# Tuned linear attention and a feed-forward layer on one core: a third group of the first product goes to seven quarter products, two of its sums share one pair of PSUM banks, q is loaded in longer runs, and the order of the work is a written list

## The chip, the core and the metric

The kernel runs on one core of a Trainium2 chip. Times are device microseconds (us) of that core, from one launch to its end; the figure that counts is the median of several runs. A profiled execution gives, beside its own time, a trace: the span from its first to its last instruction, with every instruction of the engines in it. The engines are PE (matrix products; PEld is its weight load), DVE (vector), ACT (scalar), POOL and SP. POOL and SP mostly issue DMAs here. Each engine works through its instructions in order, and a wait at one instruction holds up all behind it on that engine.

## What is computed

Eight batches with eight heads of 576 tokens and 64 channels go through attention without a softmax, then a normalization, then two matrix products with a leaky step between them. Cut to what matters:

```python
kv  = einsum('bhsd,bhse->bhde', k, v)            # q, k, v: (8, 8, 576, 64)
o   = einsum('bhsd,bhde->bhse', q, kv)
x   = (o / sqrt(mean(o*o, -1) + 1e-6) * g_norm)  # heads side by side: (4608, 512)
h   = x @ w_in                                   # the first product, 512 -> 2048
g   = maximum(h, 0) + alpha * minimum(h, 0)      # the gate
out = g @ w_out                                  # the second product, 2048 -> 512
```

## The kernel before

The 4608 tokens are cut into nine blocks of 512, w = 0 to 8. Blocks 0 and 1 are written out as straight code. From block 2 on every piece of work is a step: `put_m1`, `put_attention`, `put_m2`, `put_moves` and `put_rest` (L1450 to L1760) list them with what they need, and `in_order` (L1875) emits them. Before the change it takes, of the steps that are ready, the one with the lowest due time in the table `AT` (L1774). The order in which steps are emitted is the order of the instructions on every engine, since the pools are under a manual schedule.

The first product has 16 output tiles of 128 features in a block, in four groups s = 0 to 3. A plain tile (`put_tile`, steps M, r, s) is four matmuls of 512 columns into one PSUM bank (L641), then ACT writes relu(-h) to `m_sb` (L650), then DVE forms the gated result `gt` (L656). A fast group (`put_fast`, from block 3 on for s = 2 and 3) makes the four tiles of a group with seven products of quarters instead of eight (steps f.w.s.n): each is four matmuls of 256 columns (L1247). Products 1, 6, 7 and 4 are summed in a bank Y, 2 in a bank X, 5 and 3 in a bank V. Between them ACT copies the state of Y: `seed` (into X, before 6 changes Y), `u2` (after 6) and `u3` (after 7). DVE forms the other two quarters as `c22` = V + u3 after product 5, and `c12` = V + u2 after product 3 (L1269), both into tiles `mh` in SBUF. All four quarters are then gated 256 columns at a time: ACT copy (L1307), two DVE steps (L1314). The sums of quarters of x and w_in that the products need are the steps t and a.

Four banks serve the first product: h1 and h2 of one pool, m0 and m1 of another, each m bank a tile of its own. They go round: a fast group takes Y, V and X from the list `hs`, which is then turned over, so that the next group gets other banks.

The second product (steps p, L895) uses seven quarter products over sums of `gt` (steps S); a step p is four matmuls of 256 columns. Steps y read its banks, steps st store the result.

For attention, POOL issues the loads of k, v and q (steps ld). Each load is preceded by a one-element copy on POOL, a gate (L1402), that waits for a recent `gt`, so that loads don't start too early. q comes in four loads of 128 tokens (`load_q`, L209), each in runs of 64 channels; SP turns each by a DMA transpose (steps q, L400) into `qt_sb`. Steps kv and kvc make the per-head matrix; steps R (L519) make the rows of o, q2 and q3 their squares on ACT, rs the root, n the scaling on DVE, x the transpose by SP into `xt` for the next block. SP also issues some stores of results.

The last block ends with the second product's last quarter and its stores.

Of the kernel before, what the change touches and what calls it, by code (L numbers as in the profile page):

```python
# [17 lines left out]
def kernel(  # L18
# [11 lines left out]
    nc = tc.nc  # L30
# [178 lines left out]
    def load_q(b, t):  # L209
        if (b, "q") not in stages:  # L210
            stages[b, "q"] = stage_for(b, "q", [P, TPP, H, D])
        nc.gpsimd.dma_start(  # L212
            out=stages[b, "q"][:, t, :, :],
            in_=srcs["q"][b, :, t * P : (t + 1) * P, :].rearrange("h p d -> p h d"),
        )
# [176 lines left out]
    def dma_t(b, ts=tuple(range(NT))):  # L392
        qt = qt_sb[b % 2][:, :, PAD : PAD + S]
        for t in ts:
            c0, c1 = t * P, min((t + 1) * P, S)
            if t == TPP:
                src = rem_of(b, "q")[0:REM]
            else:
                src = buf_of(b, "q")[:, t] if b < B_NAT else stages[b, "q"][:, t]
            nc.sync.dma_start_transpose(  # L400
                out=qt[:, :, c0:c1], in_=src.rearrange("p h d -> p (h d)"),
            )
        for j in range(NPAIR):
            qts[b, j] = qt_sb[b % 2][:, j, PAD : PAD + S]

# [99 lines left out]

    def rows_mm(w, tiles):
        o_ps = row_tile([2, 2, NPAIR, D], "or_ps")
        for x, i in enumerate(tiles):
            b, r = divmod(w * W + i * P, S)
            for j in range(NPAIR):  # L510
                if r + P <= S:
                    steps = ((b, PAD + r),)
                else:
                    assert r + PAD == S
                    steps = ((b, S), (b + 1, 0))
                for n, (bb, c) in enumerate(steps):
                    for h in range(2):
                        part = slice(h * D, (h + 1) * D)
                        nc.tensor.matmul(  # L519
                            out=o_ps[:, h, x, j, :],  # L520
                            lhsT=qt_sb[bb % 2][part, j, c : c + P],
                            rhs=kvs[bb, j][part, part],
                            start=(n == 0), stop=(n == len(steps) - 1), skip_group_check=True,
                        )
            ots[w, "r", i] = o_ps[:, :, x]
# [100 lines left out]
    gt_last = []  # L626
    h_turn = [0]
# [72 lines left out]
    def row_pieces(n0):  # L700
        i = 0
        while i < P:
            b, r = divmod(n0 + i, S)
            np_, nt = (P0, T0) if b == 0 else (P, TPP)
            if b < B_NAT and r < np_ * nt:
                t, p = divmod(r, np_)
                cnt = min(P - i, np_ - p)
                yield i, cnt, b, t, p
            else:
                cnt = P - i if b >= B_NAT else min(P - i, S - r)  # L710
                yield i, cnt, None, n0 + i, 0
            i += cnt
# [186 lines left out]
    def quad_out(w, r, h, src, subs=(0, 1)):  # L899
        n0 = w * W + r * HW  # L900
        if n0 >= B_NAT * S and len(subs) == 2:
            put(
                out[n0 : n0 + HW, h * HC : (h + 1) * HC].rearrange("(a p) m -> p a m", p=P),
                src[:],
            )
            return
# [286 lines left out]
    M1_FROM = {2: 3, 3: 3}  # L1193
    HD = NC // 2
    spare, xsums, m1s = {}, {}, {}
    SPARE = {1: "q", 2: "k", 3: "v"}
    hs = ["h2", "h1", "m0", "m1"]
# [10 lines left out]
    def a_sum(s, n, pool=0):  # L1208
        if s not in spare:
            spare[s] = stage_tile(SPARE[s], [P, 4, HD, 2 * P])  # L1210
# [48 lines left out]
    def m1_step(w, s, what, tags):  # L1259
# [7 lines left out]
        elif what in ("c22", "c12"):  # L1267
            src, u = (t["V"], t["u3"]) if what == "c22" else (t["V"], t["u2"])
            nc.vector.tensor_add(out=h_tile(t, what)[:, :, HW:W], in0=src[:], in1=u[:])  # L1269
        elif what in ("a11", "a21"):  # L1270
            src = t["X"] if what == "a11" else t["Y"]
            nc.scalar.copy(out=h_tile(t, what)[:, :, 0:HW], in_=src[:])
        elif what[1] in "AB":
            i = s + (what[1] == "B") * KQ
            r = int(what[2])
            h = t["h" + what[1]]
            if what[0] == "r":
                t["m" + what[1:]] = m_new(h[:, r, :])
                return
            m1_out(w, i, r, slice(0, W), t["m" + what[1:]][:], h[:, r, :])  # L1280
            gt_add(w, i, 2)
        else:
            f_half, t_half = int(what[1]) - 1, int(what[2]) - 1
            cols = slice(t_half * HW, (t_half + 1) * HW)
            if t_half == 0:
                h = t["X" if f_half == 0 else "Y"][:]
            else:
                h = t["hB" if f_half else "hA"][:, :, HW:W]
# [3 lines left out]
            i = s + f_half * KQ  # L1292
# [4 lines left out]

    def h_tile(t, what):
        nm = "hA" if what in ("c12", "a11") else "hB"
        if nm not in t:  # L1300
            t[nm] = u_p.tile([P, 2, W], FP32, name="mh", bufs=2)
        return t[nm]
# [7 lines left out]
    def m1_out(w, i, r, cols, m, h):  # L1310
        if (w, i) not in gts:
            gts[w, i] = gt_tile(w, i)
        g = 2 * i + r
        nc.vector.scalar_tensor_tensor(  # L1314
            out=gts[w, i][:, r, cols], in0=m, scalar=beta_sb[:, g : g + 1], in1=h,
            op0=ALU.mult, op1=ALU.add,
        )
        gt_last[:] = [gts[w, i][0:1, r, cols.start : cols.start + 1]]
# [26 lines left out]
    def kv_copy(b):  # L1345
        for i in range(2):
            part = slice(i * D, (i + 1) * D)
            nc.scalar.copy(out=kv_masked[part, b % 4, :, part], in_=kv_tiles[b][part])
# [77 lines left out]
    def load(nm, b):  # L1426
        if nm == "q":
            for t in range(TPP):
                load_q(b, t)
# [7 lines left out]
    planned.append(1)  # L1437

# [21 lines left out]
    def put_fast(w, s):  # L1460
        tags = dict(Y=hs[0], V=hs[1], X=hs[2])
        hs[:] = [hs[3], hs[2], hs[1], hs[0]]
# [18 lines left out]
        do("c22", "tt", key("u3"), key(5), take=("h", w, s, "B"))  # L1481
        mm(3, key("c22"), ("a", s, 4))
        do("c12", "tt", key(3), key("u2"), take=("h", w, s, "A"))
        done = {}
        for half, p1, p2, n in (("A", "11", "12", 2), ("B", "21", "22", 4)):
            old_gt = ("gt", w - 2, s + KQ * (half == "B"))
            if whole(w, s, half):
                do("a" + p1, "copy", key(n), key("c" + p2))
                for r in range(2):
                    m = ("m", w, s, half, r)  # L1490
                    do(f"r{half}{r}", "relus", key("c" + p2), key("a" + p1), take=m)
                    do(f"s{half}{r}", "stt", key(f"r{half}{r}"), old_gt,
                       free=(m, ("h", w, s, half)) if r else (m,))
                done[half] = key(f"s{half}0"), key(f"s{half}1")
                done[p1] = key("a" + p1)
            else:
                for x, p in enumerate((p1, p2)):
                    m = ("m", w, s, p)
                    do("r" + p, "relus" if x else "relu", key("c" + p2) if x else key(n), take=m)
                    do("s" + p, "stt2", key("r" + p), old_gt, free=(m, ("h", w, s, half)) if x else (m,))  # L1500
                done[half] = key("s" + p1), key("s" + p2)
                done[p1] = key("s" + p1)
        bank_free[tags["Y"]] = done["21"], key(4)
        bank_free[tags["V"]] = (key("c12"),)
        bank_free[tags["X"]] = (done["11"],)
# [31 lines left out]
    def put_m2(w):  # L1537
# [17 lines left out]

        full = lambda f, k: f(k) + f(k + 1) if pairs else f(k)
        for k in range(0, 4, 2 if pairs else 1):
            if w > 1:
                sums(3, k, *full(lo, k), *used(7, k))
            sums(1, k, *full(lo, k), *full(hi, k), *used(5, k))  # L1560
            sums(2, k, at(1, k), *used(6, k))
# [105 lines left out]
    def put_rows(w, tiles, free, used):  # L1667
        needs = []
        for i in tiles:
            b, r = divmod(w * W + i * P, S)  # L1670
            needs += [("q", b, t) for t in range(r // P, min((r + P - 1) // P, TPP) + 1)]
            needs.append(("kvc", b))
            if r + P > S:
                needs += [("q", b + 1, 0), ("kvc", b + 1)]
# [16 lines left out]
    def put_moves(w):  # L1691
        b = w + 1
        for t in range(NT if b < B else 0):
            step(("q", b, t), "turn", lambda t=t: dma_t(b, (t,)),
                 (("ld", "q", b, t), *(("R", b - 1, i) for i in (1, 3))))
# [5 lines left out]
    def turned(what, w, i):  # L1701
        if what == "x":
            return xts[w][0:1, 0, i * P : i * P + 1]
        return qt_sb[w % 2][0:1, 0, PAD + i * P : PAD + i * P + 1]
# [7 lines left out]
    def put_load(nm, b):  # L1712
        needs = (("kv", b - 1),) if nm != "q" else ()
        for t in range(NT) if nm == "q" else (TPP, 0):
# [12 lines left out]
            own = (("q", b - 2 if t == TPP else b - 1, t),) if nm == "q" else ()  # L1727
            step(("ld", nm, b, t), "part" if t == TPP else "loadq" if nm == "q" else "load", fn, needs + own + after)

    def put_rest():  # L1730
# [12 lines left out]
        for w in range(min(M1_FROM.values()), NW):  # L1743
            for n in range(1, 5):
# [3 lines left out]
                     (*x_all(w), *((("t", w, n // 2),) if n in (2, 4) else ()), *used))  # L1748

    LATE_KV = 4  # L1750

    def whole(w, s, half):
        return False
# [23 lines left out]
    LOOP = 27.0  # L1777
    AT = {
# [160 lines left out]
```

## Time and profile before

| | us |
|---|---|
| median of the runs | 272.12 |
| the runs | 271.74, 274.9, 272.12 |
| the profiled execution's own time | 270.98 |
| its span | 269.2 |
| PE busy | 261.9 |
| DVE busy | 228.1 |
| ACT busy | 191.8 |
| POOL busy | 94.9 |

The 1.8 us between own time and span lie before the first and after the last instruction. A busy time counts the union of an engine's instructions. [...] In a timeline row stand the start, the length, engine and line, the tile written and the tiles read, and the number of equal instructions in the row; in brackets the idle time before it and what ended that.

### The profile page before, as it was taken

How to read it: one execution, taken by the hardware profiler on the slowest of the kernel's cores; microseconds unless marked ns; L12 is line 12 of the kernel's file. 1: busy time of each engine (PE TensorE's matmuls, PEld its weight loads, DVE VectorE, ACT ScalarE, POOL GpSimd, SP SyncE). 2: the span in 40 equal slices, each digit the busy share in tenths (PEclk: the TensorE clock that was granted, in tenths of full speed). 3: DMA queues.
4: the chain of work that ended last, by engine and by line, in shares of the span. 5: the costliest groups of instructions: out<-in, count | busy, mean ns of one | idle time of the engine just before them, and what ended most of it. 6: DMA issues, size and time to landing. Idle time of an engine off the chain costs nothing.

```text
span 269.2 us, 6788 instructions
## 1 busy us (share of the span) xinstructions
PE 261.9 (97%) x2477; PEld 182.8 (68%) x2477; DVE 228.1 (85%) x437; ACT 191.8 (71%) x684; POOL 94.9 (35%) x166
## 2 busy tenths in 40 slices
PE   6999999999999999999999999999999999999994
PEld 2554454456556757885788678867885788678883
DVE  6559966899977888999889988998899989978962
ACT  2567637787579779879977997799779983757400
POOL 8853652513530326874346521804040003002100
PEclk9999999999999999999999999999999999999999
DMA  7999999995999899999999993999464013100413
GB/s 189 201 199 206 195 198 189 183 195 92 195 128 169 75 131 126 129 161 197 189 163 156 138 153 66 110 191 129 107 138 99 19 24 119 39 2 11 145 41 118
DMA packets 90821, 35.76 MB, mean 133 GB/s; under 512 B 62996, under 2 KB 88612, under 8 KB 90788
## 3 DMA queue, kind: packets, MB, share of 16 engines
q0 software_dynamic: 57104, 23.68, 68.5%
q1 hardware_dynamic: 32708, 10.63, 24.0%
q10 hardware_dynamic: 976, 1.02, 1.2%
q8 instruction: 19, 0.31, 0.5%
q14 instruction: 14, 0.11, 0.2%
HBM read 36.71 MB, written 9.44 MB: 171 GB/s over the span
## 4 chain that ended last, share of the span: by engine, by line
PE 85%; DMA 8%; ACT 2%; issue 2%; DVE 1%; SPq 1%; POOL 0%; POOLq 0%
PE h_ps L641 23%; PE yY L895 14%; PE yX L895 9%; PE yZ L895 8%; PE mY L1247 8%; PE y L686 5%; PE mV L1247 4%; DMA qt_sb<-qst 3%; PE h_ps L674 2%; DMA vst<-in_v_dram 2%; PE mX L1247 2%; PE or_ps L519 1%; DMA y_sb<-in_g_norm_dram 1%; DMA qst<-in_q_dram 1%; PE kv_ps L1337 1%
## 5 line engine op out<-in xcount | busy, mean ns | idle before, releaser
L641 PE MATMUL h_ps<-xt,w_in_sb 128*128 128x512 f16 x348 | 83.0, 379 | 0.1
L656 DVE SCALAR_TENSOR_TENSOR gt<-m_sb,beta_sb,h_ps 128x512 f16<-128x512 f32 x96 | 67.1, 741 | 4.6 <-ACT m_sb L650 3.6
L650 ACT ACTIVATE m_sb<-h_ps 128x512 f32<-128x512 f32 x96 | 55.0, 604 | 14.3 <-PE h_ps L641 11.9
L641 PEld LDWEIGHTS <-w_in_sb 128*128 128x128 f16 x348 | 33.1, 98 | 32.3 <-issue 0.3
L895 PEld LDWEIGHTS <-s 128*128 128x128 f16 x496 | 48.0, 98 | 8.4 <-DVE s L813 0.2
L895 PEld LDWEIGHTS <-gt 128*128 128x128 f16 x384 | 37.4, 98 | 8.6
L582 ACT ACTIVATE sq_sb<-or_ps 128x64 f16<-128x64 f32 x192 | 39.7, 286 | 2.2 <-PE or_ps L519 2.2
L582 ACT ACTIVATION_READ_ACCUMULATOR sq_sb<-or_ps 128x1 f32 x192 | 39.4, 273 | 0.0
L1402 POOL COPY gate_sb<-gt 1x1 f16<-1x1 f16 x39 | 10.5, 269 | 76.9 <-DVE gt L656 54.7
L895 PE MATMUL yX<-w_out_sb,gt 128*128 128x256 f16 x256 | 35.2, 273 | 0.0
L895 PE MATMUL yY<-wsum,s 128*128 128x256 f16 x256 | 32.9, 273 | 0.0
L698 POOL DMA_DIRECT2D out_dram<-y_sb x24 | 15.2, 639 | 45.8 <-ACT y_sb L957 42.8
L608 DVE TENSOR_TENSOR x_rows<-or_ps,rstd_r 128x512 f16<-128x512 f32 x27 | 17.4, 685 | 9.0 <-ACT rstd_r L592 8.8
L1314 DVE SCALAR_TENSOR_TENSOR gt<-m_sb,beta_sb,mh 128x256 f16<-128x256 f32 x48 | 20.5, 477 | 0.2 <-ACT m_sb L1307 0.2
L1307 ACT ACTIVATE m_sb<-mh 128x512 f32<-128x512 f32 x24 | 15.1, 629 | 6.3 <-DVE mh L1269 6.3
L1266 ACT COPY mu<-mY 128x512 f32<-128x512 f32 x24 | 14.1, 588 | 6.5 <-PE mY L1247 6.5
L1269 DVE TENSOR_TENSOR mh<-mV,mu 128x512 f32<-128x512 f32 x24 | 16.4, 685 | 2.5 <-ACT mu L1266 2.4
L212 POOL DMA_DIRECT2D qst<-in_q_dram x20 | 17.8, 891 | 2.2 <-issue 2.0
L686 PE MATMUL y<-w_out_sb,gt 128*128 128x512 f16 x64 | 16.3, 380 | 0.0
L895 PE MATMUL yZ<-wsum,s 128*128 128x256 f16 x120 | 16.2, 273 | 0.0
L895 PE MATMUL yY<-wsum,gt 128*128 128x256 f16 x128 | 15.5, 273 | 0.0
L1247 PEld LDWEIGHTS <-w_in_sb 128*128 128x128 f16 x144 | 14.1, 98 | 1.6
(150 smaller groups left out, 425.0 us busy)
## 6 DMA issues: line engine op xcount, KB each, us to landing
kst<-in_k_dram POOLq DMA_DIRECT2D x7, 512.0 KB, 7.7
vst<-in_v_dram POOLq DMA_DIRECT2D x6, 512.0 KB, 6.5
out_dram<-y_sb POOLq DMA_DIRECT2D x11, 256.0 KB, 3.2
qst<-in_q_dram POOLq DMA_DIRECT2D x20, 128.0 KB, 4.5
w_out_sb<-in_moe_w_out_dram POOLq DMA_DIRECT2D x8, 256.0 KB, 12.1
out_dram<-y_more POOLq DMA_DIRECT2D x5, 256.0 KB, 4.2
w_in_sb<-in_moe_w_in_dram POOLq DMA_DIRECT2D x2, 512.0 KB, 10.4
qst<-in_q_dram POOLq DMA_DIRECT2D x2, 512.0 KB, 10.7
```

The costliest lines, as they stand in the source:

```text
L212: nc.gpsimd.dma_start(out=stages[b, "q"][:, t, :, :], in_=srcs["q"][b, :, t * P : (t + 1) * P, :].rearrange("h p d -> p h d"),)
L582: nc.scalar.activation(out=sq[:, half, j], in_=o_ps[:, half, j], func=AF.Square, accum_out=ssq[:, half, j : j + 1],)
L608: nc.vector.tensor_tensor(out=xr[:].rearrange("p j h d -> p h j d"), in0=o_ps, in1=rstd[:].unsqueeze(3).to_broadcast([P, 2, NPAIR, D]), op ...
L641: nc.tensor.matmul(out=h_ps[:], lhsT=w_in_blk(c, g), rhs=xts[w][:, c, :], start=(c == 0), stop=(c == NC - 1),)
L650: nc.scalar.activation(out=neg[w, g][:], in_=h_ps[:], func=AF.Relu, scale=-1.0)
L656: nc.vector.scalar_tensor_tensor(out=gts[w, i][:, r, :], in0=neg.pop((w, g))[:], scalar=beta_sb[:, g : g + 1], in1=h_ps[:], op0=ALU.mult, ...
L686: nc.tensor.matmul(out=y[:], lhsT=gt_cols(w, g, a * P, (a + 1) * P), rhs=w_out_blk(g), start=(n == 1), stop=(n == NF),)
L698: engs[store_turn[0] % len(engs)].dma_start(out=dst, in_=src)
L895: nc.tensor.matmul(out=bank, lhsT=lhs, rhs=rhs, start=fresh, stop=(c == NK - 1), skip_group_check=True,)
L1247: nc.tensor.matmul(out=t[bank][:, r, :], lhsT=lhs[:, c, r * P : (r + 1) * P], rhs=rhs[:, c, :], start=(fresh and c == r == 0), stop=(c == ...
L1269: nc.vector.tensor_add(out=h_tile(t, what)[:, :, HW:W], in0=src[:], in1=u[:])
L1314: nc.vector.scalar_tensor_tensor(out=gts[w, i][:, r, cols], in0=m, scalar=beta_sb[:, g : g + 1], in1=h, op0=ALU.mult, op1=ALU.add,)
```

## The change

1. `M1_FROM = {1: 4, 2: 3, 3: 3}`: group 1 is made by seven products too, in blocks 4 to 8. Five times 16 matmuls of 512 columns give way to 28 of 256, with the copies and sums of a fast group. The sums of w_in for it get a tile of their own.
2. The banks m0 and m1 become the two halves of one tile, allocated once: `m_pair`, 128 x 2 x 512. In every fast group X is m0 and V is m1; Y takes h2 and h1 in turn. Plain tiles on m0 or m1 write halves of the same tile.
3. `c12` is written back into the V half in PSUM. X and V side by side then hold both quarters of a result tile, and one ACT copy and one DVE step of 512 columns, which reach into both banks (steps rA0, sA0, rA1, sA1), gate it. `c22`, 21 and 22 are as before, with a smaller `mh`.
4. q of batches 3 to 7 is loaded in two loads of four heads, in the layout of k and v (each partition holds four tokens that follow each other, 512 bytes in a run after the cast). A transpose takes two heads with all their tokens, so the rows of one tile need all four transposes. A second copy of the per-head matrix with the halves swapped is made by `kvc` (three ACT copies instead of two). Rows where two batches meet are made in parts of 64. Outputs are stored by the new token order, in more and smaller pieces.
5. A written list `ORDER` of all steps takes the place of due times and planner. A load in it carries its gate (`@name`), or none (`@!`).

```diff
-    def load_q(b, t):
-        ...
-            out=stages[b, "q"][:, t, :, :],
-            in_=srcs["q"][b, :, t * P : (t + 1) * P, :].rearrange("h p d -> p h d"),
+    QL = 2
+    def load_q(b, i):
+        load_main(b, "q", i * H // QL, (i + 1) * H // QL)
...
     def m1_bank(tag, shape, name):
-        pool = ps_h if tag[0] == "h" else m_pool[0]
-        return pool.tile(shape, FP32, name=name, tag=tag)
+        if tag[0] == "h":
+            return ps_h.tile(shape, FP32, name=name, tag=tag)
+        bank = m_pair[:, int(tag[1])]
+        return bank if len(shape) == 2 else bank.rearrange("p (r n) -> p r n", r=shape[1])
...
-    M1_FROM = {2: 3, 3: 3}
+    M1_FROM = {1: 4, 2: 3, 3: 3}
-    hs = ["h2", "h1", "m0", "m1"]
+    hs = ["h2", "m0", "m1", "h1"]
...
-        elif what in ("c22", "c12"):
-            src, u = (t["V"], t["u3"]) if what == "c22" else (t["V"], t["u2"])
-            nc.vector.tensor_add(out=h_tile(t, what)[:, :, HW:W], in0=src[:], in1=u[:])
+        elif what == "c22":
+            t["h"] = u_p.tile([P, 2, HW], FP32, name="mh", bufs=2)
+            nc.vector.tensor_add(out=t["h"][:], in0=t["V"][:], in1=t["u3"][:])
+        elif what == "c12":
+            nc.vector.tensor_add(out=t["V"][:], in0=t["V"][:], in1=t["u2"][:])
+        elif what[1] == "A":
             r = int(what[2])
+            h = m_pair[:, :, r * HW : (r + 1) * HW]
             if what[0] == "r":
                 t["m" + what[1:]] = m_new(h)
                 return
+            m1_out(w, s, r, slice(0, W), t["m" + what[1:]][:], h)
...
+    m_pair = m_pool[0].tile([P, 2, W], FP32, name="m_pair")
...
     def put_fast(w, s):
-        tags = dict(Y=hs[0], V=hs[1], X=hs[2])
-        hs[:] = [hs[3], hs[2], hs[1], hs[0]]
+        tags = dict(Y=hs[0], X="m0", V="m1")
+        hs[:] = hs[::-1]
...
+        for r in range(2):
+            m = ("m", w, s, "A", r)
+            do(f"rA{r}", "relu", key("c12"), key(2), take=m)
+            do(f"sA{r}", "stt", key(f"rA{r}"), old_gt, free=(m,))
...
+        bank_free[tags["V"]] = bank_free[tags["X"]] = done["A"]
...
             def fn(t=t, after=after):
-                gate(gt_last[0])
+                for src in load_gate:
+                    gate(src)
```

A stretch of the list, in block 7, where the pair of banks goes from group 2 to group 3:

```python
f.7.2.3 f.7.2.r21 f.7.2.2 f.7.2.c12 x.8.2 f.7.2.r22 p.6.5.0 n.8.3 p.6.5.1 f.7.2.rA1 p.6.2.3
f.7.2.rA0 f.7.2.sA1 x.8.3 p.6.5.2 f.7.3.1 f.7.2.sA0 p.6.5.3 f.7.2.s22 f.7.3.seed f.7.3.5
y.6.c11 f.7.3.6
```

Steps f with a number, p, M, R and kv are PE's; seed, u, r and most y are ACT's; c, s, t, S and n are DVE's; x and q are SP's, ld POOL's.

More of the change, by code (lines that the diff above doesn't have):

```diff
@@ L402, in dma_t, with qt_flat, place_of @@
             )
-        for j in range(NPAIR):
+        for j in range(NPAIR if b < B_NAT else 0):
             qts[b, j] = qt_sb[b % 2][:, j, PAD : PAD + S]
+    def qt_flat(b):
+        return qt_sb[b % 2][:].rearrange("p j n -> p (j n)")
+    def place_of(b, r):
+        if b >= B_NAT and b % 2:
+            r = r - REM if r >= REM else r + MAIN
+        return divmod(r, P) if r < MAIN else (TPP, r - MAIN)
     def unit0(i):
@@ L506, in rows_mm @@
     def rows_mm(w, tiles):
         o_ps = row_tile([2, 2, NPAIR, D], "or_ps")
+        ops = [row_ops(w, i) for i in tiles]
+        apart = all(len({y[0] for y in x}) == 1 for x in ops)
+        left = []
         for x, i in enumerate(tiles):
[L509 to L524, printed above, removed]
@@ L525, in rows_mm @@
-            ots[w, "r", i] = o_ps[:, :, x]
+            half = ops[x][0][0]
+            ots[w, "r", i] = o_ps[:, half] if apart else o_ps[:, :, x]
+            left += [(x, *op) for op in ops[x]]
+        if not apart:
+            left.sort(key=lambda y: y[3].stop - y[3].start)
+        was = None
+        while left:
+            n = next((n for n, y in enumerate(left) if was and y[1] != was[1]), 0)
+            x, half, h, rows, j, lhs, rhs = was = left.pop(n)
+            nc.tensor.matmul(
+                out=ots[w, "r", tiles[x]][rows, h, j, :], lhsT=lhs, rhs=rhs, start=True,
+                stop=True, skip_group_check=True,
+            )
@@ L1427, in load @@
         if nm == "q":
[L1428 to L1429 removed]
+            for i in range(QL):
+                load_q(b, i)
             load_rem(b, "q")
@@ new lines @@
+    """.split()
+    def in_order():
+        todo = {".".join(map(str, s[0])): s for s in steps if s[1]}
+        names, done, gates = {s[0] for s in steps if s[1]}, set(), {"-": gt_last[0]}
+        for x in ORDER:
+            name, _, at = x.partition("@")
+            s = todo.pop(name)
+            assert all(n in done or n not in names for n in s[3]), name
+            if at:
+                load_gate[:] = [gates[at]] if at != "!" else []
+            yield s[2]
+            done.add(s[0])
+            gates[name] = gt_last[0]
+        assert not todo
```

347 lines of the change are left out of this document (203 added, 144 removed), and 66 rows, old and new, of the table AT.

## The prediction

> **What bounds the kernel now.** I read the busy times, then the chain, then busy times by block, then single rows.
>
> ```profile
> PE 261.9 (97%) x2477; PEld 182.8 (68%) x2477; DVE 228.1 (85%) x437; ACT 191.8 (71%) x684; POOL 94.9 (35%) x166
> PEclk9999999999999999999999999999999999999999
> PE 85%; DMA 8%; ACT 2%; issue 2%; DVE 1%; SPq 1%; POOL 0%; POOLq 0%
> ```
>
> PE fills the span, and the chain that ended last runs on it for 85%, at full clock throughout. What PE saves is saved, and what PE waits is lost. Next the blocks 3 to 7 (PE, PEld, DVE, ACT, POOL in each stretch):
>
> ```profile
> 117.50:144.80 27.30, 26.75 (x272) 20.65 (x268) 24.07 (x46) 23.01 (x99) 14.05 (x27) 1.00 1.28 163
> 144.80:171.80 27.00, 27.00 (x278) 20.81 (x276) 24.88 (x47) 23.02 (x99) 11.52 (x23) 1.00 0.95 116
> 171.80:199.00 27.20, 27.20 (x286) 20.95 (x284) 24.92 (x47) 23.12 (x99) 7.99 (x14) 1.00 0.92 131
> 199.00:226.40 27.40, 27.40 (x248) 21.26 (x247) 26.01 (x49) 23.17 (x98) 2.65 (x4) 1.00 0.32 84
> ```
>
> A block takes about 27 us and PE has no gap, but DVE idles only 1.4 to 3.2 us and ACT about 4 us in each. This order works because every wait is covered exactly. How exactly, one place shows:
>
> ```profile
> 106.89 0.60 PE L1247 MATMUL mY<-t,kst 128*128 128x256 f16 x4
> 107.33 1.04 PE L895 MATMUL yY<-wsum,s 128*128 128x256 f16 x8
> 107.53 0.59 ACT L1266 COPY mu<-mY 128x512 f32<-128x512 f32 x1
> 108.20 0.60 PE L1247 MATMUL mY<-t,kst 128*128 128x256 f16 x4
> 116.28 0.68 DVE L1269 TENSOR_TENSOR mh<-mV,mu 128x512 f32<-128x512 f32 x1
> 117.00 0.63 ACT L1307 ACTIVATE m_sb<-mh 128x512 f32<-128x512 f32 x1 [1.30 <-DVE mh L1269]
> 117.53 0.58 ACT L1307 ACTIVATE m_sb<-mY 128x512 f32<-128x512 f32 x1
> 117.73 0.88 DVE L1314 SCALAR_TENSOR_TENSOR gt<-m_sb,beta_sb,mh 128x256 f16<-128x256 f32 x2 [0.17 <-ACT m_sb L1307]
> 118.14 0.60 PE L1247 MATMUL mV<-xt,vst 128*128 128x256 f16 x4
> 118.78 0.69 DVE L1269 TENSOR_TENSOR mh<-mV,mu 128x512 f32<-128x512 f32 x1 [0.17 <-PE mV L1247]
> 107.01 1.41 DVE L656 SCALAR_TENSOR_TENSOR gt<-m_sb,beta_sb,h_ps 128x512 f16<-128x512 f32 x2
> 113.39 0.60 ACT L1266 COPY mu<-mY 128x512 f32<-128x512 f32 x1
> 113.87 0.61 ACT L957 COPY y_more<-yX 128x512 f32<-128x512 f32 x1
> ```
>
> Product 6 (106.89) hands over at 107.33 and its copy u2 is done at 108.12; product 7 starts at 108.20. The eight matmuls between cover 0.87, and nothing is lost. From these rows I take the hand-over times: the end of PE's record is 0.16 after its next matmul starts (0.60 against a step of 0.44); PE to DVE or ACT 0.04 (118.74 to 118.78); DVE to ACT 0.04 (116.96 to 117.00); ACT to DVE 0.10 (117.63 to 117.73); ACT or DVE to PE about 0.05. Two ACT copies in a row start 0.48 apart, two DVE gating steps 0.67 (1.41 less 0.74).
>
> **PE's work.**
>
> ```profile
> L656 DVE SCALAR_TENSOR_TENSOR gt<-m_sb,beta_sb,h_ps 128x512 f16<-128x512 f32 x96 | 67.1, 741 | 4.6 <-ACT m_sb L650 3.6
> L650 ACT ACTIVATE m_sb<-h_ps 128x512 f32<-128x512 f32 x96 | 55.0, 604 | 14.3 <-PE h_ps L641 11.9
> L1314 DVE SCALAR_TENSOR_TENSOR gt<-m_sb,beta_sb,mh 128x256 f16<-128x256 f32 x48 | 20.5, 477 | 0.2 <-ACT m_sb L1307 0.2
> L1269 DVE TENSOR_TENSOR mh<-mV,mu 128x512 f32<-128x512 f32 x24 | 16.4, 685 | 2.5 <-ACT mu L1266 2.4
> L1266 ACT COPY mu<-mY 128x512 f32<-128x512 f32 x24 | 14.1, 588 | 6.5 <-PE mY L1247 6.5
> 103.76 1.89 PE L641 MATMUL h_ps<-xt,w_in_sb 128*128 128x512 f16 x8
> 110.82 1.91 PE L895 MATMUL yY<-wsum,gt 128*128 128x256 f16 x16
> L641 PE MATMUL h_ps<-xt,w_in_sb 128*128 128x512 f16 x348 | 83.0, 379 | 0.1
> L895 PE MATMUL yX<-w_out_sb,gt 128*128 128x256 f16 x256 | 35.2, 273 | 0.0
> ```
>
> Eight wide matmuls take 1.89 with the last record's 0.379, so they are 0.216 apart; narrow ones (1.91 - 0.273)/15 = 0.109. Five blocks lose 80 wide ones and gain 140 narrow: 80 x 0.216 - 140 x 0.109 = 2.0 us less. **-2.0**, on the path.
>
> **The other engines.** DVE: a plain group costs 4 x 0.74 = 2.96. A fast group cost 2 x 0.685 + 8 x 0.477 = 5.2 and now, with two steps of 512, 2 x 0.685 + 2 x 0.74 + 4 x 0.477 = 4.8. Five more fast groups add 9, the twelve old ones give back 5, four sums of w_in add under 2: +6 in all. ACT: 3 x 0.588 + 4 x 0.60 for 4 x 0.604, five times, is +9, and five more copies of kv +2. Both lie beside PE in blocks of which DVE idles 1.4 to 3.2 and ACT 4: **0**. Without that cover it would be about 1 us in each of five blocks, a rival below.
>
> **Loads and queues.** 20 loads of q become 10 and their packets a quarter; POOL drops 23 of 39 gate copies and gains some ten small stores, at 0.6 to 0.9 us each; SP keeps its transposes in another order.
>
> ```profile
> vst<-in_v_dram POOLq DMA_DIRECT2D x6, 512.0 KB, 6.5
> kst<-in_k_dram POOLq DMA_DIRECT2D x7, 512.0 KB, 7.7
> 72.98 5.15 SPq L400 DMA_TRANSPOSE qt_sb<-qst  x4
> 72.98 4.52 DMA qt_sb<-qst
> 128.17 0.53 PE L519 MATMUL or_ps<-kv_masked,qt_sb 64*128 64x64 f16 x24 [0.55 <-issue]
> 99.83 1.24 PE L641 MATMUL h_ps<-xt,w_in_sb 128*128 128x512 f16 x5
> 101.22 0.41 PE L519 MATMUL or_ps<-kv_masked,qt_sb 64*128 64x64 f16 x16
> ```
>
> The tightest loads are v of batches 4 and 5 and k of 7: 11 to 12 us of PE's work lie between their place in the list and the kv that reads them, against 6.5 to 7.7 to land: 0. Two waits of R for q go: 0.55 at 128.17, and 0.25 before 101.22 (five matmuls from 99.83 are spent by 100.91). The new list has q turned 8 us and more ahead there: **-0.8**. The first R of block 3 now waits for the second transpose after the late stores instead of the first: 1.29 later on SP. It would land between 76.8 and 78.8, with PE there at about 76.5; before, it waited 0.5. Bounds -0.4 and +2.0; with lighter loads around it I take **+0.2**.
>
> **The bank pair.** This decides. m0 and m1 are now one tile, and in the built program every access of one engine to it is ordered behind the earlier ones of other engines, whichever half they touch. Three things follow from the waits in the program. DVE's first gating step (sA) waits for both ACT copies (rA). Where seed stands ahead of product 5, product 5 (half m1) waits for seed (half m0). Product 2 (m0) waits for c22 (which reads m1) where c22 stands ahead of it, and c12 waits for product 2 where that stands ahead.
>
> So after product 3 the next user of the pair waits for: PE's end 0.16, to DVE 0.04, c12 0.685, to ACT 0.04, two copies 0.48 + 0.60, to DVE 0.10, two steps 0.67 + 0.74, to PE 0.05, together 3.56. With a seed in between (0.04 + 0.59) it is 4.19, and 0.44 more where c12 waits for product 2. PE's cover is what stands between in the list, 0.437 for a step f or p. In block 7 from f.7.2.3 to f.7.3.5 stand f.7.2.2, five p and f.7.3.1, seven steps, 3.06; the need is 4.19 + 0.44 = 4.63, a stall of 1.57. From f.5.1.3 to f.5.2.6 stand eight steps, 3.49, for a need of 4.19: 0.70. Done for all sixteen hand-overs, by block 3 to 8: 0.5, 2.2, 2.3, 2.1, 3.0, 1.8, together **+12.0**. Before, the next group had its V and Y in other banks, and only X waited, for one step of DVE.
>
> Product 7 to c22 takes 0.16 + 0.04 + 0.59 + 0.04 + 0.685 + 0.05 = 1.57. The list covers 0.87 (f.4.3, f.5.3) or 1.31 (f.5.2, f.7.1, f.7.2, f.8.2) before the product that waits for it: 2 x 0.70 + 4 x 0.26 and 0.1 elsewhere, **+2.6**. Their ends: nothing if PE happens to be late there, and 15 if all of it holds; I take all, since before exactly such sums fit the rows to 0.05.
>
> No row of before shows a copy or a step that reaches into two banks, nor DVE writing PSUM. I price them by the same shapes in one bank, 0.60, 0.74 and 0.685; they are on the chain above, so 10% more on them costs about 3 us, 10% less gives it back.
>
> **Sum.** 270.98 - 2.0 - 0.8 + 0.2 + 12.0 + 2.6 = 283.0 by the profiled execution's own time. The median of the runs stood 1.14 above it, so 284.1.
>
> **Rivals.** (A) The pair costs no more than the list allows: copies and steps alternate (rA, sA beside the other rA), the halves are free of each other. The need falls by one copy's 0.48 to 3.07, against covers of 2.84 to 3.97; of the stalls 1.5 stay at the hand-overs and 0.8 at c22. 270.98 - 2.0 - 0.8 + 0.2 + 2.3 = 270.7, or 271.8: not slower. It decides from the point where the need is at most about 3.1. For it: in the rows of before, where the banks are tiles of their own, product 7 and the sums beside it cost PE nothing. Against: the waits stand in the built program.
>
> (B) Only the order of copies before steps binds, not that across the halves. Need 3.56 and 4.19 without the seed for product 5 and the 0.44: 6.8 and 0.8. 270.98 - 2.0 - 0.8 + 0.2 + 7.6 = 276.0, or 277.1. [...]
>
> (C) DVE becomes the bound as well: in the stretch to 226.4 it idles 1.4 us, and a block gets 1 us more of it. If PE's new stalls do not give it air, since they come while PE waits for DVE itself, up to 1 us in each of four blocks more: 288.
>
> **How the numbers follow.** The forecast has 0.66, A 0.10, B 0.12, C 0.12. 2%, about what a measurement can tell from no change, is 277.6 or 266.7. The forecast and C are slower; B lies at the edge, half of it slower; A is the same. So slower 0.83, same 0.15, faster 0.02, for A with every cover holding (269.5) and something more. The range leaves out A and the low half of B, and reaches to C: 276.5 to 288. The likeliest alone has 280 to 288.
>
> **What would show it.** PE's busy time in blocks 4 to 8 falls below its stretch, with idle before L1247 put down to DVE gt or ACT m_pair, 0.3 to 1.6 us each, and before product 2 put down to DVE mh. The two steps of 512 show DVE waiting for the second ACT copy. The wait at R near 128 is gone. If L1247 shows no idle on the pair, the step "bank pair" is wrong; if the idle is there but half as long, the waits across halves are.

## The result, and the profile after

The changed kernel takes 304.49 us (median of six runs, 303.71 to 305.3), the kernel before, run beside it, 272.48; the ratio is 1.116, 95% interval 1.111 to 1.121. It is slower, as forecast, but by 32 us where the forecast said 12, and it lies above the range's upper end of 288. The profiled execution took 304.55 with a span of 302.8, so the sums below are made against 304.55 and against the 270.98 of before: 33.6 to explain.

The page of the changed kernel: PE's and DVE's busy time, the granted clock in 40 slices, and the chain that ended last.

```profile
PE 270.9 (89%) x2537; PEld 190.4 (63%) x2537; DVE 233.0 (77%) x437; ACT 202.1 (67%) x704; POOL 83.1 (27%) x143
PEclk9999999999999899999999999599999999999999
PE 36%; DVE 25%; ACT 18%; DMA 12%; issue 5%; SPq 3%; POOL 0%; DVEq 0%; ACTq 0%; POOLq 0%
```

Before, the chain ran on PE for 85%. Now it hops between PE, DVE and ACT, and for 12% it lies on transfers. One slice ran at about half clock and one at 0.8. Who waits for whom on PE (us in total, times, longest):

```profile
PE mY L1292 <- ACT m_pair L1308: 5.9, 9, 1.6
PE m_pair L1292 <- ACT m_pair L1308: 5.9, 6, 1.4
PE m_pair L1292 <- DVE mh L1314: 5.1, 4, 4.0
PE h_ps L722 <- DMA xt<-x_rows: 2.0, 1, 2.0
```

L1308 is the seed (ACT writes m0), L1314 is c22, both on the bank pair. These two lines carry the first three rows; 4.0 of the third has another cause, the second one below. The view puts a wait down to the last instruction of a chain, so a single place has to be followed to see what the seed itself waited for. From product 3 of group 2 to product 5 of group 3 in block 7 (timeline of PE, DVE, ACT: start, duration):

```profile
246.55 0.60 PE L1292 MATMUL m_pair<-xt,kst 128*128 128x256 f16 x4
246.99 0.60 PE L1292 MATMUL m_pair<-xt,w_in_sb 128*128 128x256 f16 x4
249.61 0.60 PE L942 MATMUL yZ<-wsum,s 128*128 128x256 f16 x4
251.59 0.60 PE L1292 MATMUL m_pair<-t,vst 128*128 128x256 f16 x4 [1.39 <-ACT m_pair L1308]
247.62 0.70 DVE L1316 TENSOR_TENSOR m_pair<-m_pair,mu 128x512 f32<-128x512 f32 x1 [0.53 <-PE m_pair L1292]
249.48 1.41 DVE L1351 SCALAR_TENSOR_TENSOR gt<-m_sb,beta_sb,m_pair 128x512 f16<-128x512 f32 x2 [0.56 <-ACT m_sb L1341]
248.36 1.09 ACT L1341 ACTIVATE m_sb<-m_pair 128x512 f32<-128x512 f32 x2 [0.56 <-DVE m_pair L1316]
250.97 0.57 ACT L1308 COPY m_pair<-mY 128x512 f32<-128x512 f32 x1 [1.53 <-DVE gt L1351]
```

The chain goes product 3 (246.55, PE free again at 246.99), product 2, sum c12 (247.62), two copies (248.36), two gating steps (249.48), seed (250.97), product 5 (251.59). Product 5 writes the half m1 and the seed the half m0, and still one waits for the other. From 246.99 to 251.59 are 4.60; the forecast's working had 4.63 for this place and a stall of 1.57, and PE lost 1.55 (251.59 less 249.61 less the 0.44 of four products is 1.54; the rest is rounding).

The second new thing is a different one (timelines of SP, POOL, PE, DVE, with one piece of the chain that ended last in the second row; then two stretches with the granted clock in the last column but two):

```profile
88.63 3.46 SPq L665 DMA_TRANSPOSE xt<-x_rows  x2
90.88 6.66 DMA xt<-x_rows
90.34 0.92 POOL L204 DMA_DIRECT2D vst<-in_v_dram  x1
97.58 0.45 PE L722 MATMUL h_ps<-xt,w_in_sb 128*128 128x128 f16 x4 [2.00 <-DMA xt<-x_rows]
181.58 1.43 SPq L665 DMA_TRANSPOSE xt<-x_rows  x1
190.36 0.42 DVE L1276 TENSOR_TENSOR t<-xt 128x512 f16<-128x512 f16 x1 [3.55 <-DMA xt<-x_rows]
190.70 0.69 DVE L1314 TENSOR_TENSOR mh<-m_pair,mu 128x512 f32<-128x512 f32 x1
191.44 1.01 PE L1292 MATMUL m_pair<-xt,w_in_sb 128*128 128x256 f16 x4 [4.05 <-DVE mh L1314]
```

```profile
97.60:101.40 3.80, 3.80 (x13) 1.54 (x13) 1.08 (x2) 0.60 (x1) 0.24 (x1) 0.55 1.68 165
191.40:197.00 5.60, 5.56 (x27) 3.60 (x27) 3.16 (x6) 1.09 (x2) 0.00 (x0) 0.52 0.10 24
```

Twice the last transposed rows of a block land late: at 97.5 for an issue at 90.88, and at about 190.3 (the sum that waits starts at 190.36) for one at 181.58. In block 3 PE waits for them itself, 2.00. In block 6 DVE does, 3.55 for the sum t, and c22 of the block before stands behind that sum on DVE, so PE waits 4.05 for c22, which needs no transfer at all. Behind both waits the granted clock is reduced: 0.55 in the mean from 97.60 to 101.40, and 0.52 from 191.40 to 197.00.

What PE lost at each step (start of a matmul, less the start before it, less 0.216 for 512 columns or 0.109 for 256, where over 0.15), by block, beside the forecast for the hand-over behind product 3:

| hand-over | forecast | measured | hand-over | forecast | measured |
|---|---|---|---|---|---|
| 3.2 to 3.3 | 0.41 | 0.81 | 5.3 to M.6 | 0.50 | 0 (behind the wait of 4.2) |
| 3.3 to M.4 | 0.07 | 0.41 | 6.1 to 6.2 | 0.70 | 1.08 |
| 4.1 to 4.2 | 0.27 | 0.36 | 6.2 to 6.3 | 1.10 | 1.10 |
| 4.2 to 4.3 | 1.14 | 1.01 | 6.3 to M.7 | 0.29 | 0 |
| 4.3 to M.5 | 0.84 | 0.78 | 7.1 to 7.2 | 0.70 | 0.73 |
| 5.1 to 5.2 | 0.70 | 0.67 | 7.2 to 7.3 | 1.57 | 1.55 |
| 5.2 to 5.3 | 1.10 | 1.04 | 7.3 to M.8 | 0.72 | 0.88 |
| 8.1 to 8.2 | 1.14 | 1.05 | 8.2 to 8.3 | 0.70 | 0.64 |

That is 12.1 where 12.0 was forecast. Of the single forecasts the prediction gives 0.70 (5.1 to 5.2), 1.57 and the sums by block; the others follow by its rule from the list. The total agrees better than the places do: three lost 0.34 to 0.40 more (3.2, 3.3 and 6.1), and two lost nothing for 0.50 and 0.29. That these cancel is luck.

The whole account, the forecast's term in brackets: work of PE -2.0 (-2.0), waits of R for q that went -0.8 (-0.8), first R of block 3 +0.3 (+0.2), hand-overs +12.1 (+12.0), c22 +3.4, of which 0.7 lies in the wait of 4.2 (+2.6); and then what the forecast did not have: the start of group 1 behind the plain groups and a copy beside it +6.3, plain groups of block 3 on the pair +1.8, late rows +2.2 and +3.5, half clock +1.7 and +2.5, some ten small waits for ACT or DVE +2.6. The sum is 33.6.

### The profile page after: what moved, and what is told of

Same layout as the page of the kernel before. It is cut to its first block, busy times and chain, and to the rows that moved or that the text cites. A ratio compares the mean times of both kernels' runs of the same rounds, so it can differ in the third digit from the quotient of the medians.

```text
span 302.8 us, 6843 instructions
## 1 busy us (share of the span) xinstructions
PE 270.9 (89%) x2537; PEld 190.4 (63%) x2537; DVE 233.0 (77%) x437; ACT 202.1 (67%) x704; POOL 83.1 (27%) x143
## 4 chain that ended last, share of the span: by engine, by line
PE 36%; DVE 25%; ACT 18%; DMA 12%; issue 5%; SPq 3%; POOL 0%; DVEq 0%; ACTq 0%; POOLq 0%
DVE gt L1351 8%; PE h_ps L689 6%; PE m_pair L1292 6%; ACT m_sb L1341 5%; DVE gt L704 5%; PE y L734 5%; PE m_pair L689 4%; ACT sq_sb L627 4%; DMA qt_sb<-qsb 4%; PE yY L942 3%; PE mY L1292 3%; DVE m_pair L1316 3%; ACT m_sb L698 2%; DMA qsb<-in_q_dram 2%; DMA xt<-x_rows 2%
## 5 line engine op out<-in xcount | busy, mean ns | idle before, releaser
L689 PE MATMUL h_ps<-xt,w_in_sb 128*128 128x512 f16 x180 | 43.1, 379 | 0.0
L704 DVE SCALAR_TENSOR_TENSOR gt<-m_sb,beta_sb,h_ps 128x512 f16<-128x512 f32 x54 | 39.0, 744 | 5.0 <-ACT m_sb L698 4.3
L698 ACT ACTIVATE m_sb<-h_ps 128x512 f32<-128x512 f32 x54 | 31.6, 601 | 10.1 <-PE h_ps L689 5.7
L1351 DVE SCALAR_TENSOR_TENSOR gt<-m_sb,beta_sb,m_pair 128x512 f16<-128x512 f32 x34 | 24.1, 745 | 9.4 <-ACT m_sb L1341 9.4
L746 POOL DMA_DIRECT2D out_dram<-y_sb x31 | 18.3, 596 | 37.8 <-ACT y_sb L998 33.8
L1341 ACT ACTIVATE m_sb<-m_pair 128x512 f32<-128x512 f32 x34 | 18.7, 603 | 13.8 <-DVE m_pair L1316 13.2
L1292 PEld LDWEIGHTS <-w_in_sb 128*128 128x128 f16 x204 | 20.2, 99 | 10.9 <-issue 7.2
L1311 ACT COPY mu<-mY 128x512 f32<-128x512 f32 x34 | 20.1, 591 | 8.7 <-PE mY L1292 8.6
L689 PE MATMUL m_pair<-xt,w_in_sb 128*128 128x512 f16 x88 | 23.4, 401 | 2.7 <-DVE gt L1351 1.6
L746 POOL DMA_DIRECT2D out_dram<-y_more x11 | 6.6, 604 | 69.7 <-ACT y_more L998 42.0
L653 DVE TENSOR_TENSOR x_rows<-or_ps,rstd_r 128x512 f16<-128x512 f32 x27 | 18.4, 688 | 7.9 <-ACT sq_sb L627 6.0
L704 DVE SCALAR_TENSOR_TENSOR gt<-m_sb,beta_sb,m_pair 128x512 f16<-128x512 f32 x22 | 16.3, 746 | 9.7 <-ACT m_sb L698 8.2
L698 ACT ACTIVATE m_sb<-m_pair 128x512 f32<-128x512 f32 x22 | 13.0, 599 | 16.0 <-PE m_pair L689 12.9
L1316 DVE TENSOR_TENSOR m_pair<-m_pair,mu 128x512 f32<-128x512 f32 x17 | 11.9, 699 | 8.8 <-PE m_pair L1292 8.7
## 6 DMA issues: line engine op xcount, KB each, us to landing
w_out_sb<-in_moe_w_out_dram POOLq DMA_DIRECT2D x8, 256.0 KB, 12.1
```

What stands on the lines that cost most here:

```text
L653: nc.vector.tensor_tensor(out=xr[:].rearrange("p j h d -> p h j d"), in0=o_ps, in1=rstd[:].unsqueeze(3).to_broadcast([P, 2, NPAIR, D]), op ...
L689: nc.tensor.matmul(out=h_ps[:], lhsT=w_in_blk(c, g), rhs=xts[w][:, c, :], start=(c == 0), stop=(c == NC - 1),)
L698: nc.scalar.activation(out=neg[w, g][:], in_=h_ps[:], func=AF.Relu, scale=-1.0)
L704: nc.vector.scalar_tensor_tensor(out=gts[w, i][:, r, :], in0=neg.pop((w, g))[:], scalar=beta_sb[:, g : g + 1], in1=h_ps[:], op0=ALU.mult, ...
L746: engs[store_turn[0] % len(engs)].dma_start(out=dst, in_=src)
L1292: nc.tensor.matmul(out=t[bank][:, r, :], lhsT=lhs[:, c, r * P : (r + 1) * P], rhs=rhs[:, c, :], start=(fresh and c == r == 0), stop=(c == ...
```

## The experiments

The rival to the tile's ordering was that the list itself has too little cover for the chain, whatever the banks belong to. So the first edit gives the two banks back their own tiles, and the second keeps the one tile but makes every other instruction the same as in the first. The third moves two loads only, the fourth does the first and the third together.

**e1_split: two tiles, gated bank by bank**

```
-    m_pair = m_pool[0].tile([P, 2, W], FP32, name="m_pair")
+    m_pair = [m_pool[0].tile([P, W], FP32, name=f"m{i}") for i in range(2)]
...
-        bank = m_pair[:, int(tag[1])]
+        bank = m_pair[int(tag[1])][:]
...
-            h = m_pair[:, :, r * HW : (r + 1) * HW]
...
-            m1_out(w, s, r, slice(0, W), t["m" + what[1:]][:], h)
+            for r in range(2):
+                m1_out(w, s, r, slice(x * HW, (x + 1) * HW), m[:, r, :], t["XV"[x]][:, r, :])
```

Here x is 0 for the first and 1 for the second of the two copies, and the copy reads that bank alone.

> The two banks m0 and m1 are two tiles again, and the first output of a fast group is gated bank by bank, 256 wide (four DVE steps of 0.48 in place of two of 0.745 in each of 17 fast groups, +0.26 each, 4.4 us of DVE in all); order, loads and the rest are those of the changed kernel. Theory 1 (one tile for two banks orders every engine behind every other): of the PE stalls after 66 us, those at a hand-over of the pair between fast groups (12.1), at c22 (2.7), at the start of a block's group 1 (6.5) and in block 3 (2.2) go for the most part, the two waits for turned rows stay: 304.5 less about 20, 281 to 288. Rival (the list simply has too little cover for the chain product 3, sum, copies, steps, however the banks are laid out): the chain is as long, and the stalls stay, 300 to 308.

Measured: 284.32 us, ratio to before 1.0456 (1.0396 to 1.0516), 20.2 less than the changed kernel. The waits of PE that are left:

```profile
PE m L1292 <- DVE mh L1314: 3.7, 2, 3.4
PE h_ps L722 <- DMA xt<-x_rows: 3.4, 1, 3.4
PE mY L1292 <- DVE gt L704: 0.5, 1, 0.5
```

Of the two rows with the seed, 11.8 us, 0.2 is left, and the list is the same. The late rows are still there, 3.4 us each now, and nothing hides them.

**e2_pairbank: one tile, gated bank by bank**

```
+    m_pair = m_pool[0].tile([P, 2, W], FP32, name="m_pair")
...
+        bank = m_pair[:, int(tag[1])]
```

on top of e1_split, everything else as there.

> One tile for both banks stays, but the first output is gated bank by bank, 256 wide, exactly as in the run with two tiles. Theory 1 (the tile, not the width): the stalls stay and grow by the longer DVE steps, 0.26 at each of some 14 hand-overs: 304 to 309. Rival (what binds is that a step of 512 reaches into both banks): as fast as the run with two tiles, 281 to 288.

Measured: 304.88 in one run, inside the range of theory 1. The instructions on every engine are those of e1_split; 20.6 us hang on whether two banks are declared as one tile. PE waits for the seed again:

```profile
PE m_pair L1292 <- ACT m_pair L1308: 7.6, 6, 1.7
PE mY L1292 <- ACT m_pair L1308: 6.9, 9, 1.5
```

So the 512-wide step is not the cause: with the same instructions PE waits 14.5 us in these two rows with one tile for both banks and 0.2 in e1_split, where each bank is a tile of its own. The ordering across the halves was the tile's.

**e3_loads: two loads moved away from the transposes**

```
-ld.v.4.0@s.2.7 ... M.2.14 s.2.15
+M.2.14 s.2.15 ld.v.4.0@s.2.15
-ld.k.7.0@! f.5.2.c12 ... f.5.2.s22
+f.5.2.c12 ... f.5.2.s22 ld.k.7.0@f.5.2.s22
```

> Only two loads are moved: v of batch 4 is gated on the gating step of u 15 of block 2 in place of u 7 (some 5 us later), and k of batch 7, which had no gate, on step s22 of group 2 of block 5 (some 4 us later), so that neither runs beside the transposes of the last rows of blocks 3 and 6. Theory 2 (these transposes land late since a 512 KB load runs beside them, and the idle PE then loses its clock): the waits of 2.2 and 3.5 and the half clock behind them (1.7 and 2.5) go, 304.5 less 7 to 10, 294.5 to 298. Rival (they are late by the q transposes and the small stores, or by the SP queue): 302 to 306, the waits stay. A third case: kv of batch 4 or 7 then waits for its load, up to 2 us given back.

Measured: 297.03, ratio 1.0924 (1.0879 to 1.097), 7.5 less than the changed kernel. No wait of PE or DVE for these rows is left, the clock is full throughout (the page's row), and the waits on the pair stand as before (the second view):

```profile
PEclk9999999999999999999999999999999999999999
```

```profile
PE m_pair L1292 <- ACT m_pair L1308: 5.9, 6, 1.4
PE mY L1292 <- ACT m_pair L1308: 5.6, 8, 1.4
```

Of the 9.9 that the late rows and the clock had cost, about 2 came back at once as waits that they had covered (1.20 at M.3.2, 0.79 at M.6.1). The q transposes behind the rows were left as they were, so they alone are not what held the rows.

**e4_both: two tiles and the two loads moved**

The edit is that of e1_split and that of e3_loads together.

> Two tiles and the two loads moved. If both theories hold the gains add: 304.5 less 20 less 7 to 10, 273 to 279, about the time of the kernel before (272.5). If the loads' gates follow other steps in a list that runs 20 us faster, some of the second gain is lost again: up to 284.

Measured: 276.05, ratio 1.0143 (1.0095 to 1.0191). 28.4 less than the changed kernel, 20.2 and 7.5 being 27.7: the two causes add, and together they are nearly all of the loss; 4.3 us over the kernel before, run beside it (271.78), stay.

**e5_before_pair: the kernel before, with one tile for two banks**

```
-        pool = ps_h if tag[0] == "h" else m_pool[0]
-        return pool.tile(shape, FP32, name=name, tag=tag)
+        if tag[0] == "h":
+            return ps_h.tile(shape, FP32, name=name, tag=tag)
+        bank = m_pair[:, int(tag[1])]
+        return bank if len(shape) == 2 else bank.rearrange("p (r n) -> p r n", r=shape[1])
```

> The kernel before, with one edit: its banks m0 and m1 become the two halves of one tile. No instruction is added or taken away, no data goes elsewhere; only what the program orders behind what can differ. Theory 1: every writer of one half then waits for readers of the other, in each of blocks 2 to 8 at some two places by 1 to 3 us (the longest where a plain group's matmuls on one half stand behind the gating of the other): 285 to 312. Rival (the halves are free of each other on the chip and in the program, and the changed kernel stalls by its list alone): 271 to 274.

Measured: 317.21 in one run, beside 272.43 for the kernel before: 45 slower, more than the 312 at most that was expected, by a declaration alone. Three stretches of 3.41 at half clock, each behind a wait on the pair, are part of it. The long waits all name the pair; besides them there are 0.7 for `h_ps` and the two waits of the start, which the kernel before has too:

```profile
PE m_pair L643 <- DVE gt L658: 17.1, 9, 3.2
PE m_pair L1249 <- DVE gt L1316: 9.8, 6, 1.7
PE m_pair L643 <- ACT m_pair L1265: 5.3, 5, 1.8
PE m_pair L1249 <- ACT mu L1268: 4.7, 6, 1.0
```

**e6_gated_rows: the loads wait for the landing of the rows themselves**

```
+        if (nm, b) in (("v", 4), ("k", 7)):
+            return (("x", b - 1, 3),)
...
-R.3.1 p.1.7.2 q2.3.0 s.2.4 p.1.7.3
+p.1.7.2 s.2.4 p.1.7.3 R.3.1 q2.3.0
```

on top of e1_split, with the two loads placed behind x.3.3 and x.6.3 in the list.

> Two tiles as in the first experiment; v of batch 4 and k of batch 7 now wait for the landing of the transposed rows themselves (rows 3 of blocks 3 and 6), and R of the first rows of block 3 stands two products (0.87 us of PE) later. In the run with both edits kv of batch 4 lost 1.28 and that R 0.96. If the landing of v set the first (it was issued at 95.25 and took 7.8), about 1 us of it goes, and up to 0.9 of the second: 276.05 less 1.5 to 2, 274 to 275. If kv of batch 4 waits for the gating before it on DVE, only the second goes: 275.2.

Measured: 275.99, ratio 1.0134 (1.0075 to 1.0193): no gain. The wait of kv of batch 4 fell from 1.28 to 0.62 and that of the first R went, but the second R of block 3 now lost 1.08, waiting for DVE to scale the rows ahead of it (`x_rows`, L653). In both runs kv's wait names DVE (1.1 and 0.5), the expectation's second case, and R's wait only moved on.

**e7_reordered: 23 steps of the list moved**

```
-... p.1.4.0 ... R.3.3 p.1.4.1 s.2.6 q2.3.2 p.1.4.2
+... p.1.4.0 ... p.1.4.1 s.2.6 p.1.4.2 R.3.3 q2.3.2
...
 f.4.1.2, f.4.3.6, f.5.1.5, p.4.6.1, p.5.1.0, p.5.6.0, p.5.7.3, p.6.2.1, p.7.2.0, f.8.3.1: 4 to 14 places earlier
```

> The run before (two tiles, loads gated on the turned rows) with 23 of the list's steps moved by a few places: products of the second matmul stand ahead of the PE steps that waited there (c22 before product 3, the seeds of blocks 5 to 8, sums before product 6 of the last block), some copies and sums on ACT and DVE stand earlier, and R of the second rows of block 3 stands two products later. Nothing is added or removed. In the run before, waits of 0.15 to 1.1 at 22 places after 70 us add up to 8. If each is a lack of cover at its own place (what remains is the list), about 3 us go: 272 to 274, no longer slower than the kernel before by more than 0.6%. If DVE, busy 85% of the span, has become the bound, the waits only move: 275 to 276.5.

Measured: 276.81, ratio 1.0181 (1.0135 to 1.0228), no gain and a little above even the rival's 275 to 276.5. PE's losses over 0.15, counted as in the table above from 66 us on, add up to 8.1 where e6_gated_rows had 8.0: they moved. That DVE is the bound, the rival's reason, is not shown by this. DVE is fullest in the stretch from 172, which has in e6_gated_rows (PE, PEld, DVE, ACT, POOL):

```profile
172.00:199.00 27.00, 26.51 (x304) 21.36 (x296) 26.31 (x54) 25.14 (x103) 1.34 (x2) 1.00 0.48 80
```

DVE idles 0.7 us in 27 there, but only 0.8 of the 8.0 us that PE loses lie in that stretch.

**e8_plain_group1: group 1 in the plain form**

```
-    M1_FROM = {1: 4, 2: 3, 3: 3}
+    M1_FROM = {2: 3, 3: 3}
```

on top of e6_gated_rows; in the list the steps M, r, s of u 4 to 7 take the places of f.w.1, in blocks 4 to 8.

> As the run with two tiles and loads gated on the turned rows (275.99), but group 1 stays in the plain form from block 4 on (80 wide matmuls in place of 140 narrow ones; its sums of w_in are not made), its steps put where the fast ones stood in the list. Theory: the fast group is worth its 2.0 us of PE: 277 to 279. Rival: with 256-wide gating a fast group costs DVE 5.2 in place of 2.96, five times 2.2, and DVE, busy over 95% of blocks 5 to 7, is now the bound: 271 to 274.

Measured: 278.21, ratio 1.0171 (1.0111 to 1.0231), 2.2 more than e6_gated_rows. Each was run beside the kernel before at another time (272.62 and 272.43), and the intervals overlap, but the runs do not: 277.36 to 278.46 against 275.5 to 277.23. The traces agree (e6_gated_rows, then e8_plain_group1):

```profile
PE 263.3 (96%) x2537; PEld 188.5 (69%) x2537; DVE 234.1 (85%) x471; ACT 200.5 (73%) x704; POOL 84.4 (31%) x142
PE 265.2 (96%) x2477; PEld 182.7 (66%) x2477; DVE 224.5 (81%) x437; ACT 193.4 (70%) x689; POOL 83.8 (30%) x142
```

PE is busy 1.9 longer and DVE 9.6 less, and PE's losses over 0.15 stay at 8.1, beside 8.0. So the fast form of group 1 does earn the 2.0 of PE that its matmuls save, once the banks are free; the rival, that DVE eats it, falls. Taking load from DVE alone gained nothing in this list.

**e9_pool_sums: two sums of x on POOL**

```
     def pool_x(w, n):
-        return False
+        return n in (3, 4)
```

on top of e6_gated_rows.

> As the run with two tiles and loads gated on the turned rows (275.99), but two of the four sums of x of each block (those for products 7 and 4) are made by POOL, busy 30%, in place of DVE: 2 x 0.34 x 6 = 4 us less on DVE. If DVE sets what is left of the waits, 272.5 to 275; if the waits sit on single chains, 275.5 to 276.5; if POOL's sum is late (no row shows one; its DMA issues take 0.6 to 0.9 each and stand in the same queue), 277 to 282.

Measured: 281.24, ratio 1.0289 (1.0195 to 1.0383), 5.3 more. The groups of e6_gated_rows, then those of e9_pool_sums (busy, mean ns):

```profile
L1278 DVE TENSOR_TENSOR t<-xt,t 128x512 f16<-128x512 f16 x6 | 2.5, 415 | 0.1
```

```profile
L1278 DVE TENSOR_TENSOR t<-xt,t 128x512 f16<-128x512 f16 x6 | 5.9, 989 | 0.1
L862 DVE TENSOR_TENSOR s<-gt 128x1024 f16<-128x1024 f16 x14 | 11.2, 806 | 0.0
L1282 POOL TENSOR_TENSOR t<-xt,t 128x512 f16<-128x512 f16 x6 | 8.5, 1420 | 2.4 <-PE m L689 1.5 <-issue 0.8
L1280 POOL TENSOR_TENSOR t<-xt 128x512 f16<-128x512 f16 x6 | 7.2, 1194 | 13.7 <-DVE t L1276 13.6
```

A sum that takes DVE 0.42 takes POOL 1.2 to 1.4, and while it runs some of DVE's own 16-bit sums take longer: 0.989 for 0.415 at L1278 in the mean. Four of these six ran beside a sum of POOL and took 0.49 to 1.94; the other two took 0.42. DVE's busy time rose (239.2 from 234.1) with twelve instructions fewer. The time lies in the third range, but POOL's own lateness is the smaller part: 0.9 of PE's waits name a sum of POOL, and the longest, 1.5, name DVE.

No version beat the kernel before; the best, 275.99 and 276.05, are 1.3 and 1.4% slower.

## Why the prediction went wrong, point by point

**Where it was right.** That the bank pair decides: shown by e1_split, e2_pairbank and e5_before_pair, each a change of what counts as one tile. The size at the places that were worked out: 12.1 for 12.0, and 3.4 for 2.6 at c22. PE's work: -2.0 forecast, and about 2 is what the fast group earned in e8_plain_group1. The prices that no row of before showed: a copy and a step over two banks took 0.603 and 0.745 against 0.60 and 0.74 in one bank, and DVE's sum written into PSUM 0.699 against 0.685.

```profile
L1351 DVE SCALAR_TENSOR_TENSOR gt<-m_sb,beta_sb,m_pair 128x512 f16<-128x512 f32 x34 | 24.1, 745 | 9.4 <-ACT m_sb L1341 9.4
L1341 ACT ACTIVATE m_sb<-m_pair 128x512 f32<-128x512 f32 x34 | 18.7, 603 | 13.8 <-DVE m_pair L1316 13.2 <-DVE gt L1351 0.6
L1316 DVE TENSOR_TENSOR m_pair<-m_pair,mu 128x512 f32<-128x512 f32 x17 | 11.9, 699 | 8.8 <-PE m_pair L1292 8.7
```

**Step "Loads and queues", 0: failed, worth 9.9.** It priced a load by whether it lands before its own reader, 11 to 12 us against 6.5 to 7.7, and did not ask what the load does to the transposes that run beside it. The two rows that decide landed after 6.7 and 8.7. v of batch 4 was issued half a microsecond ahead of its row, k of batch 7, which had lost its gate, 2.1 ahead, and beside them ran the smaller stores. In e3_loads the two loads are issued 4.1 and 4.0 behind the rows, and the waits and the half clock are gone. The medians would not have told it: 2.9 from issue to landing before, 3.7 now, and 4.1 in e4_both, where neither PE nor DVE waits for a turned row. But the trace of before held the price. Two rows turned at 82.45 and 83.73, behind the loads of v and k of batch 4 (issued at 78.14 and 79.79), took 7.3 in the median, the next ones 2.5; PE and DVE did not wait for them then (windows 82:85 and 88.5:91 of before):

```profile
xt<-x_rows SPq DMA_TRANSPOSE x2, 7.3
xt<-x_rows SPq DMA_TRANSPOSE x2, 2.5
```

Of the stores and of q's longer runs no run was made alone.

**Step "The bank pair", the list of sixteen hand-overs: too short, worth 8.1.** It followed the pair from product 3 to its next user. But in the plain groups, too, the banks of the pair change hands, by a copy and a step each, and the seed and the products of group 1 stand right behind them: 1.72 at block 6, 1.61 at block 8, 1.29 at block 4 (0.93 and 0.36), 0.77 at block 5, and 0.90 at block 7, where a copy of the second product comes late. The same ordering holds in block 3, between plain tiles (0.91, 0.57) and at the first product behind them (0.35). The mechanism was the forecast's; the count of places was not complete. In e4_both each of these places loses 0.52 at most.

**Step "The other engines", 0: mis-sized, worth about 2.6.** Some ten waits of 0.16 to 0.6 for a copy of ACT or a sum of DVE, among them 0.39 for u3 of block 2 and 0.52 and 0.57 in the last block, stand in the changed list and not in the old one. In the versions with two tiles they make up most of what is left, and in e7_reordered moving 23 steps only moved them. Which of them come from the list and which from DVE's load is open; e8_plain_group1, with 9.6 us less on DVE and as much lost on PE, speaks against DVE's load alone.

**The clock, taken as full: failed, worth 4.2**, counted in the 9.9 above. Before, the granted clock fell only at the very end (0.98 in the stretch from 253.00), 3.2 us after PE's last product, and from 66 us on PE's longest idle time between its products was 0.55; the changed kernel's idle times, 2.00 and 4.05 at the two falls of the clock, were not priced for it.

**The rivals.** A (no cost of the pair) is refuted by e2_pairbank against e1_split. B (only copies before steps) is refuted by the table: from 7.2 to 7.3, where the seed and product 2 made the forecast's need 4.63 and B's 3.56 against a cover of 3.06, B gives 0.50 at product 5 and PE lost 1.55 there. C (DVE binds as well) is not borne out: with the pair as one tile DVE idles 23%. With two tiles it idles 0.7 in 27 in its fullest stretch, but e8_plain_group1 took 9.6 us from DVE and gained nothing, so what the last 1.3% waits for stays open.

## What to carry to other kernels

Count a tile that spans two banks as one resource (20.6 us between e1_split and e2_pairbank): before joining two banks, list every pair of neighbouring accesses by different engines, plain groups included, and give each the whole chain of hand-overs. When a load is moved or loses its gate, price the transposes beside it (7.5 us in e3_loads), and look which in-order engine has other work queued behind the one that waits. An engine that looks idle in the mean (POOL at 30%) is no place for a sum before its duration and its effect on DVE have been measured (5.3 us lost in e9_pool_sums).

## What the runs showed of the hardware

In the changed kernel TensorE's granted clock is half from 97.76 to 101.17 and from 189.92 to 196.75, for 3.41 and 6.83, and full for the 88.75 between; these are 1, 2 and 26 times 3.413. Stretches of that length, counted from a change of the clock (length, PE's busy time, the granted clock in the last column but two; the second half-clock row is two such lengths; two rows of the changed kernel, four of e1_split, one of e2_pairbank):

```profile
94.35:97.76 3.41, 1.41 (x14) 1.00 1.32 229
97.76:101.17 3.41, 3.41 (x12) 0.50 1.78 168
94.01:97.42 3.41, 1.12 (x9) 1.00 1.39 187
97.42:104.24 6.82, 5.76 (x17) 0.50 0.91 103
179.34:182.75 3.41, 1.71 (x16) 1.00 1.47 125
182.75:186.16 3.41, 1.69 (x14) 1.00 1.01 160
187.49:190.90 3.41, 1.43 (x14) 1.00 1.41 123
```

PE was busy for 1.41 and 1.12 in the stretch ahead of the two falls in these rows, that is idle for 2.0 and 2.3, and for 0.88 in the one ahead of the changed kernel's fall at 189.92. The idle time of 3.4 at 181 us of e1_split was as long as the one at the rows, but it lay across two stretches, each busy for 1.7, and the clock stayed full. It stayed full behind the 1.43 of e2_pairbank too, and in the changed kernel behind every other full-clock stretch up to the last products, the least busy of which had 1.85. Half clock ended after a stretch that PE filled (3.41); where PE began one idle (until 191.44, and until 98.48 in e1_split) it lasted a second one. What sets a fall was not tried by a run of its own.

A transposing transfer of rows that landed 2.4 us after its issue where little else ran (at 213.78 in the changed kernel) took 6.7 and 8.7 beside a load of 512 KB, and 7.3 in the median beside two of them before. And where POOL made 16-bit sums between SBUF tiles (e9_pool_sums above), four of DVE's six at L1278 took 0.49 to 1.94 for 0.42; POOL's took 1.194 and 1.420 in the mean. The steps that read PSUM hardly changed (L1354 on the two banks 474 ns in e6_gated_rows and 475 in e9_pool_sums), while L1354 on the tile `mh` in SBUF went from 477 to 528.
